# A fused attention, MoE and feed-forward kernel: weight decoding loaded two steps ahead, its mask on POOL, and token transposes spread over PSUM banks

## The chip, the cores and the metric

The kernel runs on one core of one Trainium2 chip. The metric is the device time of one execution in microseconds (us). TensorE appears as PE (matmul) and PEld (loading of the stationary operand), VectorE as DVE, ScalarE as ACT, GpSimd as POOL and the engine that issues most transfers as SP. Each of them works through its own instructions in the order in which they were written; semaphores hold an instruction back until its operands and its buffer are there.

## The reference, cut to what matters

Three layers follow one another on 2304 tokens of 512 values: windowed attention, a top-2 mixture of 8 experts, and a feed-forward layer with a piecewise gate. The change touches only what surrounds the last two.

```python
def _moe_ref(x, w_gate, w_noise, noise, w1, w2):        # N, D = 2304, 512; E, F = 8, 1024
    ...
    for e in range(E):
        for k in range(2):
            mask = top2[:, k] == e
            ...
            h = np.maximum(x[mask] @ w1[e], 0.0)
            out[mask] += top2_w[mask, k, None] * (h @ w2[e])

def _moe2_ref(x, w_in, w_out):                          # 512 -> 2048 -> 512
    h = x @ w_in
    g = np.where(h >= 1, h, np.where(h <= -1, 0.0, (h + 1) ** 2 / 4.0))
    return g @ w_out
```

The two matrices of the last layer, `w_in` and `w_out`, arrive as 64-bit floats. [...]

## The kernel before, in words

**Stages.** Attention comes first (to about 107 us of the span), with the router's choice of experts. Then the experts run one after another, each with up to 640 tokens that a gather by POOL brings in: unit 0 and 1 (one expert in two parts), units 2 to 7 (one expert each, called e1 to e6; the sorted lists get shorter, from 640 to 544 tokens), a small unit of 64 spilled tokens (`SPILL`), and units 7a and 7b. Last come five groups of the feed-forward layer, g0 with 256 tokens and g1 to g4 with 512 each. g0 multiplies plainly (`plain`); from g1 on each block is computed by a scheme with seven products in place of eight (`wino`), for which sums of blocks of `w_in` were prepared and stored earlier.

**A step.** Inside an expert the loop runs over 8 chunks of the hidden layer. PE computes `mm1` of the next chunk (L863) and then `mm2` of this one (L926). Matmuls run with 32-bit values cut in a high and a low part, three products for each. So for every chunk ACT writes the high part and DVE the rest, of the hidden values (`act_relu`: ReLU at L871, subtraction at L874) and of the weights (`split_w`: L157, L158). `mm1` writes into two PSUM banks; the next `mm1` may start when L871 and L874 have read them. The transpose of the next expert's tokens (L743 on PE, L746 and L747) goes between the two.

**Decoding.** While units 2 to 6 run, seven of every eight steps also decode 128x512 numbers, 32 pieces in all. `dec_load` (L174, SP) brings the raw integers into one of two buffers `rawd`. `dec_a` makes a mask `dm` on ACT that is positive where the number is not too small (L182 Abs, L183 Sign). `dec_b` has five DVE operations (L195, L197, L199, L200, L201), of which L199 takes the larger of mask and zero and multiplies by it, and a POOL addition (L203) that writes `td`. In the loop `dec_a` is issued ahead of the next chunk's `mm1` and its ReLU; `dec_b` and the next `dec_load` come at the end of the step, and the load of piece i+1 is issued in the step that decodes piece i.

**Sums and stores.** After every fourth piece a list `todo` gets ten entries: four POOL sums (L220, in two entries) and eight splits (L236 on ACT, L237 on DVE). `prepare(3)` in each step issues the stores of what is ready (L246, SP) and then three entries. The tiles of these sums, the masks, the gathered tokens and the results that are scattered all rotate through one pool `sc` with ten buffers.

**From g0 to g1.** The tokens of the next group are two rows each, y1 and y2 (one per chosen expert). `prep_mix` scales both on ACT (L1027, L1028) and adds them on POOL (L1029). `xcopy` transposes 128 tokens with four PE operations (L1222), always into bank 7 (`TR`), and ACT copies them out (L1226). `xsums` (L1236) and `xsplit` (L1245, L1246) make the operands of `wino`, and the table `AT` says at which place of a step: entry (p, j) is step p of the group and position j of seven. The gate of g0 (`act_gate`: L881 to L888) goes back and forth between ACT and DVE for each of two chunks.

What follows are the functions that the change touches and those that call them.

## Time and profile before

| what | value |
|---|---|
| three timed runs | 999.34, 999.82, 1005.02 us (median 999.82) |
| the profiled execution | 992.05 us, of which the span from first to last instruction is 990.3 us |
| PE, PEld busy | 950.4 us (96%), 841.4 us |
| DVE, ACT, POOL busy | 656.5 us (66%), 441.7 us (45%), 223.7 us (23%) |
| mean granted TensorE clock | 0.988 of full speed |
| moved by DMA | 201 MB, mean 203 GB/s |

A busy PE says that matmuls are under way, not that they run at their best speed. A row "idle before X <- Y" says how long the engine of X stood before it and which event ended that. The granted clock is given as a share of full speed: 1.00 is the upper of the two levels (2.4 GHz) and 0.50 the lower (1.2 GHz).

### The profile page before, as it was taken

How to read it: one execution, taken by the hardware profiler on the slowest of the kernel's cores; microseconds unless marked ns; L12 is line 12 of the kernel's file. 1: busy time of each engine (PE TensorE's matmuls, PEld its weight loads, DVE VectorE, ACT ScalarE, POOL GpSimd, SP SyncE). 2: the span in 40 equal slices, each digit the busy share in tenths (PEclk: the TensorE clock that was granted, in tenths of full speed). 3: DMA queues.
4: the chain of work that ended last, by engine and by line, in shares of the span. 5: the costliest groups of instructions: out<-in, count | busy, mean ns of one | idle time of the engine just before them, and what ended most of it. 6: DMA issues, size and time to landing. Idle time of an engine off the chain costs nothing. (4 is left out here: it accounts for less than half of the span.)

```text
span 990.3 us, 18428 instructions
## 1 busy us (share of the span) xinstructions
PE 950.4 (96%) x6917; PEld 841.4 (85%) x6918; DVE 656.5 (66%) x1386; ACT 441.7 (45%) x910; POOL 223.7 (23%) x275
## 2 busy tenths in 40 slices
PE   8998899999998989899999998899999999999998
PEld 6887789998987879789888887798899899889897
DVE  4689476586976878777442264775766676576664
ACT  6987224455564444554332254344334333433222
POOL 3212112345244344432402022112101300210000
PEclk9999999999999989989999999999999999999999
DMA  8874126568767876776927265485567558556531
GB/s 257 279 245 153 54 97 187 210 196 279 256 214 250 261 269 210 245 258 199 346 93 252 92 223 213 146 305 165 170 209 263 167 171 294 174 170 206 183 123 42
DMA packets 92796, 201.17 MB, mean 203 GB/s; under 512 B 7432, under 2 KB 17928, under 8 KB 92704
## 3 DMA queue, kind: packets, MB, share of 16 engines
q1 hardware_dynamic: 85264, 177.84, 54.6%
q0 software_dynamic: 6144, 19.76, 5.5%
q10 hardware_dynamic: 1296, 2.36, 0.6%
q8 instruction: 55, 0.90, 0.4%
q14 instruction: 37, 0.30, 0.1%
HBM read 159.65 MB, written 40.29 MB: 202 GB/s over the span
## 5 line engine op out<-in xcount | busy, mean ns | idle before, releaser
L926 PE MATMUL bank<-wo,hg 128*128 128x512 f32 x864 | 240.3, 397 | 0.0
L926 PE MATMUL bank<-w,he 128*128 128x512 f32 (+3 forms) x696 | 170.4, 396 | 0.0
L926 PEld LDWEIGHTS bank<-wo,hg 128*128 128x128 f32 x864 | 148.1, 190 | 17.6
L926 PEld LDWEIGHTS bank<-w,he 128*128 128x128 f32 (+3 forms) x696 | 124.7, 184 | 26.7
L863 PE MATMUL bank<-xhie,w 128*128 128x288 f32 (+4 forms) x768 | 125.4, 307 | 12.7 <-DVE he L874 12.7
L863 PEld LDWEIGHTS bank<-xhie,w 128*128 128x128 f32 x768 | 115.4, 194 | 21.4 <-DVE he L874 17.1
L158 DVE TENSOR_TENSOR w<-raw,w 128x1024 fp32r<-128x1024 f32 (+1 forms) x71 | 80.9, 1139 | 24.8 <-ACT w L157 24.5
L1168 PEld LDWEIGHTS bank<-xb,wi 128*128 128x128 f32 x576 | 80.4, 188 | 12.6 <-ACT r L881 2.3
L874 DVE SCALAR_TENSOR_TENSOR he<-bank,he 128x320 fp32r<-128x320 f32 (+8 forms) x120 | 43.3, 401 | 67.5 <-ACT he L871 67.4
L1168 PE MATMUL bank<-xb,wi 128*128 128x256 f32 x576 | 84.9, 283 | 2.6 <-ACT r L881 1.7
L1192 ACT ACTIVATE hg<-cg 128x512 fp32r<-128x512 f32 x64 | 40.3, 629 | 100.6 <-DVE cg L1190 100.6
L1168 PEld LDWEIGHTS bank<-xc,wi 128*128 128x128 f32 x480 | 67.2, 188 | 7.6 <-DVE wg L1153 0.6
L1168 PE MATMUL bank<-xc,wi 128*128 128x256 f32 x480 | 70.2, 281 | 0.2 <-DVE wg L1153 0.2
L157 ACT ACTIVATE w<-raw 128x1024 fp32r<-128x1024 f32 (+1 forms) x71 | 69.8, 983 | 0.0
L863 PE MATMUL bank<-xloe,w 128*128 128x288 f32 (+4 forms) x384 | 69.8, 304 | 0.0
L203 POOL TENSOR_TENSOR td<-rawd 128x512 f32<-128x512 f32 x32 | 33.3, 1039 | 158.3 <-DVE rawd L201 92.4
L871 ACT ACTIVATE he<-bank 128x288 fp32r<-128x288 f32 (+4 forms) x96 | 37.2, 412 | 65.4 <-PE bank L863 65.3
L1029 POOL TENSOR_TENSOR y<-y,y 128x512 f32<-128x512 f32 x15 | 20.5, 1363 | 200.4 <-ACT y L1028 200.4
L182 ACT ACTIVATE dm<-rawd 128x512 f32<-128x512 f32 x32 | 21.6, 675 | 90.5 <-DMA rawd<-wd 78.3
L1186 ACT ACTIVATE mg<-cg 128x512 f32<-128x512 f32 x64 | 40.1, 626 | 47.1 <-DVE cg L1158 45.4
L1187 DVE SCALAR_TENSOR_TENSOR cg<-mg,cg 128x512 f32<-128x512 f32 x64 | 47.0, 734 | 18.8 <-ACT mg L1186 18.8
L863 PEld LDWEIGHTS bank<-xloe,w 128*128 128x128 f32 x384 | 59.1, 193 | 0.0
(300 smaller groups left out, 1607.4 us busy)
## 6 DMA issues: line engine op xcount, KB each, us to landing
wi<-w1o SPq DMA_DIRECT2D x56, 1024.0 KB, 5.5
raw<-wcat SPq DMA_DIRECT2D x64, 512.0 KB, 4.3
rawd<-wd SPq DMA_DIRECT2D x32, 512.0 KB, 4.4
w1o<-so SPq DMA_DIRECT2D x64, 256.0 KB, 5.7
y<-y_dram SPq DMA_DIRECT2D x30, 256.0 KB, 5.3
vE<-v SPq DMA_DIRECT2D x18, 260.0 KB, 5.1
x_dram<-x SPq DMA_DIRECT2D x18, 256.0 KB, 2.3
k<-kT SPq DMA_DIRECT2D x8, 512.0 KB, 6.7
```

The source lines that it names most:

```text
L157: nc.scalar.activation(w[:, 0, c], t[:, c], AF.Copy)
L158: nc.vector.tensor_tensor(out=w[:, 1, c], in0=t[:, c], in1=w[:, 0, c].bitcast(F32), op=ALU.subtract)
L182: nc.scalar.activation(m, w, AF.Abs)
L203: nc.gpsimd.tensor_tensor(out=t, in0=hf, in1=lf, op=ALU.add)
L863: nc.tensor.matmul(ps, lhsT=l[k], rhs=r[:, k, s:s + w], start=(c == 0), stop=(c == len(prods) - 1))
L871: nc.scalar.activation(hh, ps, AF.Relu)
L874: nc.vector.scalar_tensor_tensor(out=t, in0=ps[:, c], scalar=0.0, in1=hh[:, c].bitcast(F32), op0=ALU.max, op1=ALU.subtract)
L926: nc.tensor.matmul(M2[b][0:w], lhsT=h2[:, o:o + w], rhs=r[n], start=(first and a == 0), stop=(last and a == end))
L1168: nc.tensor.matmul(ps, lhsT=w[:, l, k * P:k * P + P], rhs=r[:, m, k, :], start=(c == 0), stop=(c == len(prods) - 1))
L1186: nc.scalar.activation(st["m"], c, AF.Relu, scale=0.5)
L1187: nc.vector.scalar_tensor_tensor(out=c, in0=st["m"], scalar=1.0, in1=c, op0=ALU.min, op1=ALU.subtract)
L1192: nc.scalar.activation(h2[:, 0:T], c, AF.Copy, scale=-1.0)
```

## The change

The diff has five parts.

1. **Loads of the decoding.** Three `rawd` buffers in place of two. The first two pieces are loaded at the end of unit 1, and every decoding step begins with the stores that are ready and the load of piece i+2. `dec_a` is issued after the next chunk's `mm1` and ReLU.
2. **The mask.** ACT gets a third operation, a ReLU of the mask, so that it is 0 or 1. The DVE operation L199 is gone; POOL multiplies the finished piece by the mask in a second operation behind its addition. So ACT has one operation more for each of 32 pieces, DVE one fewer, POOL one more.
3. **Sums and stores.** Their tiles have a pool of their own, `so`, with six buffers. `todo` gets four entries per four pieces, one for each step, and every sum is split one step after POOL was told to make it.
4. **The weight ring** has 10 buffers in place of 12. The last two of the four pairs of the spill unit's chunks and two of the four `wi` tiles use a pool `we` in the place that the decoding's pools leave; those are closed in unit 7, not in `SPILL`. The last pair is loaded at chunk 5, not 4.
5. **From g0 on.** Transposes of even blocks go into bank 7, those of odd blocks into one of banks 2 to 6 that the group at work doesn't use. For g1 alone the mix is one ACT scaling and one DVE operation. The first two splits for g1 no longer wait for the sums and stand at (4, 0) and (4, 2).

```diff
-RING = 12
-PAIRS = (0, 1, 3, 4)
+RING = 10
+PAIRS = (0, 1, 3, 5)
...
+    def stream(k, shape, dt, name):
+        return ring.tile(shape, dt, tag="w", name=name) if k < 2 else pool["we"].tile(shape, dt, tag=f"w{k}", name=name)
+
     def load_raw(n, eng=nc.sync):
         if SP <= n < NCE:
 
             if n % 2 == 0:
-                pool["pair"] = ring.tile([P, 2, 1024], F32, tag="w", name=f"w{n}")
+                pool["pair"] = stream((n - SP) // 2, [P, 2, 1024], F32, f"w{n}")
...
         nc.scalar.activation(m, w, AF.Abs)
         nc.scalar.activation(m, m, AF.Sign, bias=tiny[:, 0:1])
+        nc.scalar.activation(m, m, AF.Relu)
         d64[i] = (d64[i], m)
 
     def dec_b(i):
...
-            nc.vector.scalar_tensor_tensor(out=hf, in0=m, scalar=0.0, in1=hf, op0=ALU.max, op1=ALU.mult)
...
             nc.gpsimd.tensor_tensor(out=t, in0=hf, in1=lf, op=ALU.add)
+            nc.gpsimd.tensor_tensor(out=t, in0=t, in1=m, op=ALU.mult)
...
         def add(j, x, y, op):
-            o[j] = pool["sc"].tile([P, 2, 256], F32, tag="s", name=f"so{p}_{j}")
+            o[j] = pool["so"].tile([P, 2, 256], F32, tag="so", name=f"so{p}_{j}")
...
-        todo.extend((first, second))
-        for j, src in ((5, None), (2, None), (3, None), (6, None), (0, a11), (1, a12), (4, a22), (7, a21)):
-            todo.append(lambda j=j, src=src: split(j, src))
+        def cut(*js):
+            for j in js:
+                split(j, {0: a11, 1: a12, 4: a22, 7: a21}.get(j))
+        todo.extend((lambda: (first(), cut(0, 1)), lambda: (second(), cut(5, 2)), lambda: cut(3, 6), lambda: cut(4, 7)))
...
             nc.scalar.activation(y1, y1, AF.Copy, scale=wts[:, t, 0:1])
-            nc.scalar.activation(y2, y2, AF.Copy, scale=wts[:, t, 1:2])
-            nc.gpsimd.tensor_tensor(out=y2, in0=y2, in1=y1, op=ALU.add)
+            if un is units[FIRST2 + 1]:
+                nc.vector.scalar_tensor_tensor(out=y2, in0=y2, scalar=wts[:, t, 1:2], in1=y1, op0=ALU.mult, op1=ALU.add)
+            else:
+                nc.scalar.activation(y2, y2, AF.Copy, scale=wts[:, t, 1:2])
+                nc.gpsimd.tensor_tensor(out=y2, in0=y2, in1=y1, op=ALU.add)
...
     def xcopy(ui, b):
         un = units[ui]
         t = gat.pop((un["key"], b))
+        free = [x for x in bank[2:7] if x not in units[ui - 1]["m2"]]
+        TR = bank[7] if b % 2 == 0 else free[b // 2 % len(free)]
...
         decode = 1 < ui < E - 1 and f <= 6
+        if ui == 1 and f > 5:
+            dec_load(ndl)
+            ndl += 1
+        if decode and ndl < n64:
+            prepare(0)
+            dec_load(ndl)
+            ndl += 1
...
         if ui == 1 and f == 2:
-            pool["rd"] = dec.enter_context(tc.tile_pool(name="rd", bufs=2, reuse_waits="tile"))
-            pool["td"] = dec.enter_context(tc.tile_pool(name="td", bufs=4, reuse_waits="tile"))
+            for x, k in (("rd", 3), ("td", 4), ("so", 6)):
+                pool[x] = dec.enter_context(tc.tile_pool(name=x, bufs=k, reuse_waits="tile"))
...
-        if decode and ndec < min(ndl, n64):
-            dec_a(ndec)
...
             do_mm1(ndone)
             ndone += 1
+        if decode and ndec < n64:
+            dec_a(ndec)
...
         if decode:
-            prepare(3)
-            if ndec < min(ndl, n64):
+            prepare(1)
+            if ndec < n64:
                 dec_b(ndec)
                 ndec += 1
-            if ndl < n64:
-                dec_load(ndl)
-                ndl += 1
         elif todo or stores:
-            prepare(3)
+            prepare(1)
+        if ui == SPILL - 1 and f == 2:
+            assert not todo and not stores
+            dec.close()
+            pool["we"] = ffn.enter_context(tc.tile_pool(name="we", bufs=1, reuse_waits="tile"))
...
-          {(4, 4): (None,), (4, 5): (0,), (4, 6): (1,), (5, 0): (2,), (5, 2): (3,), (5, 4): (4,), (5, 5): (5,), (5, 6): (6,)})
+          {(4, 0): (0,), (4, 2): (1,), (4, 4): (None,), (5, 0): (2,), (5, 1): (3,), (5, 3): (4,), (5, 4): (5,), (5, 6): (6,)})
```

On SP the load of the piece moves ahead of the step's weight load, and it is one piece further on. This is the step of unit 3 that has mask `dm8` on ACT (`rawd` raw integers, `raw` expert weights, `w1o` and `w2o` the stored results, `so` and `td` their tiles). Before:

```order
L174 DMA rawd8_3572<-wd 128x1024
L144 ISA
L144 DMA raw27_3634<-wcat 128x1024
L246 DMA w1o_71<-so1_5_3555 128x512
L246 DMA w2o_72<-td7_3565 128x512
L174 DMA rawd9_3651<-wd 128x1024
```

With the change:

```order
L251 DMA w1o_71<-so1_5_3462 128x512
L251 DMA w1o_71<-so1_2_3464 128x512
L251 DMA w2o_72<-td7_3539 128x512
L177 DMA rawd10_3549<-wd 128x1024
L147 ISA
L147 DMA raw26_3604<-wcat 128x1024
```

Piece 8 is now followed by the load of piece 10, still behind the stores of what was finished just before, and ahead of the weights.

On ACT, in the same step (`he` the hidden values, `w` the weight split), before:

```order
L182 ACTIVATE dm8_3576<-rawd8_3572 128x512
L183 ACTIVATE dm8_3576<-dm8_3576,tiny_110 128x512
L871 ACTIVATE he2_19_3579<-bank0_73 128x316
L871 ACTIVATE he2_19_3579<-bank1_74 128x316
L746 ACTIVATE xhie3_3608<-bank7_78 128x4x128
L157 ACTIVATE w25_3631<-raw25_3489 128x1024
```

With the change:

```order
L876 ACTIVATE he2_18_3553<-bank0_73 128x316
L876 ACTIVATE he2_18_3553<-bank1_74 128x316
L185 ACTIVATE dm8_3582<-rawd8_3307 128x512
L186 ACTIVATE dm8_3582<-dm8_3582,tiny_110 128x512
L187 ACTIVATE dm8_3582<-dm8_3582 128x512
L160 ACTIVATE w24_3601<-raw24_3448 128x1024
```

The mask has moved from ahead of the two ReLUs to between them and the weight split, and has three operations.

On PE, in step 3 of g0 (`y` the mixed tokens, `wo`, `hg` the operands of `mm2`), before:

```order
L1222 MATMUL bank7_78<-idn_164,y2_7108 128x128 x4
L926 MATMUL bank2_75<-wo3_6913,hg0_78_7187 128x512 x2
L926 MATMUL bank3_76<-wo3_6913,hg0_78_7187 128x512 x2
L1222 MATMUL bank7_78<-idn_164,y3_7111 128x128 x4
L926 MATMUL bank3_76<-wo3_6913,hg0_78_7187 128x512
```

With the change:

```order
L1232 MATMUL bank7_78<-idn_164,y2_7147 128x128 x4
L931 MATMUL bank2_75<-wo3_6952,hg0_78_7226 128x512 x2
L931 MATMUL bank3_76<-wo3_6952,hg0_78_7226 128x512 x2
L1232 MATMUL bank4_2118<-idn_164,y3_7150 128x128 x4
L931 MATMUL bank3_76<-wo3_6952,hg0_78_7226 128x512
```

The places are the same; the second block's transpose goes to bank 4.

## Rows read from the trace of the kernel before

**Rows 1.** Windows, decoding units and unit 7: us; busy PE, PEld, DVE, ACT, POOL; clock; DMA; GB/s.

```profile
225.00:466.00 241.00, 228.28 (x1315) 202.97 (x1314) 185.04 (x335) 122.03 (x238) 96.37 (x95) 0.97 0.74 243
466.00:512.00 46.00, 46.00 (x287) 40.76 (x286) 20.20 (x38) 16.18 (x29) 11.23 (x11) 1.00 0.73 250
```

**Rows 2.** Waits on PE and ACT, 225 to 466 us: total us, times, longest.

```profile
PE bank L863 <- DVE he L874: 12.7, 9, 3.3
ACT dm L182 <- DMA rawd<-wd: 64.0, 17, 7.8
```

**Rows 3.** Timeline around one stall, 302 to 307 us: start, duration, engine, instruction, idle before.

```profile
302.22 0.45 SPq L174 DMA_DIRECT2D rawd<-wd  x1
...
304.13 0.66 ACT L182 ACTIVATE dm<-rawd 128x512 f32<-128x512 f32 x1 [7.81 <-DMA rawd<-wd]
...
305.45 0.72 ACT L871 ACTIVATE he<-bank 128x304 fp32r<-128x304 f32 x2
...
306.42 1.38 PE L863 MATMUL bank<-xhie,w 128*128 128x304 f32 x8 [2.23 <-DVE he L874]
```

**Rows 4.** Windows over the three half-clock stretches of the decoding: the first, and their sum.

```profile
366.00:372.80 6.80, 5.48 (x23) 5.48 (x24) 5.50 (x11) 4.04 (x8) 1.19 (x3) 0.50 0.92 295
...
sum 13.60, PE 12.13 PEld 12.13 DVE 11.65 ACT 7.25 POOL 2.12; mean PE 4.04 PEld 4.04 DVE 3.88 ACT 2.42 POOL 0.71
```

**Rows 5.** Groups by line, 225 to 466 us: count, busy us, mean ns, idle before.

```profile
L183 ACT ACTIVATE dm<-dm,tiny 128x512 f32<-128x512 f32 x26 | 18.8, 724 | 0.8
L182 ACT ACTIVATE dm<-rawd 128x512 f32<-128x512 f32 x26 | 17.5, 674 | 76.2 <-DMA rawd<-wd 64.0 <-DVE rawd L201 6.8 <-DMA y_dram<-ye,rank_i 3.5
...
L199 DVE SCALAR_TENSOR_TENSOR rawd<-dm,rawd 128x512 f32<-128x512 f32 x27 | 18.7, 694 | 0.9
...
L200 DVE TENSOR_SCALAR td<-rawd 128x512 int32<-128x512 int32 x27 | 11.5, 427 | 0.9
...
L203 POOL TENSOR_TENSOR td<-rawd 128x512 f32<-128x512 f32 x27 | 28.1, 1039 | 130.1 <-DVE rawd L201 64.1 <-DMA raw<-wcat 18.4 <-issue 16.7
```

**Rows 6.** Transfers into the decoding's buffers, 225 to 466 us.

```profile
DMA to landing us min/median/max: 3.5/4.5/8.2
```

**Rows 7.** Timeline of a step with a late DVE, 384 to 391 us.

```profile
384.84 0.92 POOL L220 TENSOR_TENSOR so<-td,so 128x256 f32<-128x256 f32 x1
...
385.08 0.96 DVE L195 TENSOR_SCALAR td<-rawd 128x512 int32<-128x512 int32 x1
...
386.80 0.41 ACT L871 ACTIVATE he<-bank 128x288 fp32r<-128x288 f32 x1 [0.75 <-PE bank L863]
...
388.60 0.88 DVE L874 SCALAR_TENSOR_TENSOR he<-bank,he 128x288 fp32r<-128x288 f32 x3
...
390.20 1.08 PE L863 MATMUL bank<-xhie,w 128*128 128x288 f32 x7
```

**Rows 8.** Timeline of g0, 604 to 622 us: mix, transposes and their copies.

```profile
604.73 0.71 ACT L1028 ACTIVATE y<-y,wts 128x512 f32<-128x512 f32 x1
...
610.41 0.58 ACT L1226 ACTIVATE xhis<-bank 128x512 f32<-128x512 f32 x1
...
611.09 0.63 PE L1222 MATMUL bank<-idn,y 128*128 128x128 f32 x4 [3.77 <-issue]
...
621.22 0.63 PE L1222 MATMUL bank<-idn,y 128*128 128x128 f32 x4 [1.90 <-ACT xhis L1226]
```

**Rows 9.** Windows over the two half-clock stretches of g0.

```profile
611.80:615.20 3.40, 3.40 (x12) 2.85 (x11) 0.00 (x0) 2.11 (x4) 2.44 (x2) 0.50 0.00 0
622.00:625.40 3.40, 3.40 (x12) 2.81 (x11) 2.85 (x3) 1.52 (x3) 2.21 (x2) 0.50 0.12 44
```

**Rows 10.** Timeline of the end of g0, 614 to 640 us: gate on ACT, first `wino` products.

```profile
616.34 0.38 ACT L881 ACTIVATE r<-bank 128x256 f32<-128x256 f32 x1 [2.42 <-PE bank L863]
...
626.47 0.39 ACT L881 ACTIVATE r<-bank 128x256 f32<-128x256 f32 x1 [2.95 <-PE bank L863]
...
636.36 0.98 PE L1168 MATMUL bank<-xb,wi 128*128 128x256 f32 x6 [1.42 <-ACT r L881]
```

## What the change should do to the time

> **What bounds the kernel now.** I read the windows first, to see where PE stands idle. In units 3 to 6, which decode, PE is busy for 228.28 of 241 us; in unit 7, which has the same steps but no decoding, for 46.00 of 46 [rows 1]. So PE's own work sets the pace, and the decoding units lose 12.7 us on top of it. The waits say to whom: all 12.7 us, in nine waits, are an `mm1` that waits until DVE has read its bank (L874) [rows 2]. DVE was late because ACT was: over the same stretch ACT stood 64.0 us in front of the mask's first operation, waiting for the raw integers [rows 2]. The timeline shows one case from end to end: ACT idles 7.81 us before L182, only then comes the ReLU (L871) of an `mm1` that had long ended, and PE starts the next one 2.23 us late [rows 3].
>
> Idle time has a second price. After these waits come stretches in which the granted clock is 0.50, the lower level: 13.60 us in three places, with 12.13 us of matmuls in them [rows 4]. At the upper level these would take half, so the stretches cost about 12.13 / 2 = 6.1 us.
>
> The second place is g0. Two transposes of the next group's tokens wait 3.77 and 1.90 us, since bank 7 still holds the block before, which ACT copies out only at 610.41 behind the gate's long chain [rows 8]. Two stretches of 3.40 us at half clock follow [rows 9] and cost 6.80 / 2 = 3.4 us. Sum: 5.7 + 3.4 = 9.1 us. Elsewhere the change touches nothing on which PE waits noticeably.
>
> **The change, part by part.**
>
> *Loads and the place of the mask.* The raw integers land 3.5 to 8.2 us after their issue [rows 6]. The stretch of 241 us holds 32 steps; without its losses a step takes (241 - 18.8) / 32 = 6.9 us. One step ahead is therefore not enough when the load issues late, two steps (13.9 us) are. On SP the load now stands behind the stores that are ready; one of them, in every second step, waits for POOL's addition and multiplication of the piece before, 2 x 1.04 us after DVE is done with it [rows 5]. If that delays the issue by 4 us, an estimate of mine from DVE's lateness below and these 2.1 us, 9.9 us are left against at most 8.2. The weight load behind it moves later by as much, with two steps of its own in hand. And since the mask now follows the ReLU, a late load no longer holds the ReLU. So I let all nine waits go: 12.7 us, and with them the half clock, 6.1 us: 18.8 us.
>
> *What is late next.* Between ReLU and weight split ACT now has three operations: 0.674 + 0.724 us and a third that the trace lacks in this shape. Its nearest rows are those two, so 0.67 to 0.72; I take 0.70 [rows 5]. ACT's weight split, and with it DVE's half of it, the splits of the sums and the decoding, start 2.1 us later after the ReLU; DVE's part is shorter by L199, 0.694 us [rows 5]. So DVE reaches the next L874 up to 1.4 us later than now. How late may it be? In the step of [rows 7] L874 starts 1.8 us after the ReLU's start, ends at 389.48, and PE's next `mm1` starts at 390.20 without idling: 0.7 us were left, so lateness is free up to 2.5 us. A punctual L874 starts 0.4 us after the ReLU (the ReLU takes 0.41 us there); plus 1.4 makes 1.8, which is inside.
>
> *The mask on POOL.* 32 multiplications at the addition's 1.039 us [rows 5] are 33 us more on POOL, which is busy 96.37 of 241 us [rows 1]. They hide there; gathers behind them start 1 us later and have two steps. But POOL can hold DVE up: L195, which normally takes as long as its like L200, 0.427 us [rows 5], took 0.96 us while a POOL sum ran, 0.53 us more [rows 7]. One such hold leaves 0.2 us of DVE's margin, two overdraw it by 0.35 us. The multiplication follows the addition directly, when DVE is done with the piece, so it meets a DVE operation less often than the sums do. Bounds: no hold, 0 us; two holds in every one of 32 steps, 32 x 0.35 = 11 us. I take two holds in eight of the 16 steps that make sums: 2.8 us.
>
> The Trainium skill (SBUF — State Buffer, section "SBUF: two separate sides") is sterner: DVE and GpSimd take a shared port pair as an exclusive lock for a whole instruction, and the loser blocks fully. By that every multiplication may hold DVE 1.04 us, 33 us in all, and if all of it reached PE the time would be some 1010 us. The row of [rows 7] agrees that DVE stops; it shows 0.53 us for one meeting, since POOL had begun before.
>
> *Sums, own buffers, ring of 10.* One entry per step and splits a step after the sums take ACT's and DVE's waits for POOL away; they cost nothing, with the same operations as before. The stores' own six buffers relieve `sc`; a buffer of `so` is wanted again three steps after its tile was begun, one step after its store was issued. A weight buffer in a ring of 10 is written again three steps after its last use, where it was five; nobody waits. The two loads that move to the end of unit 1 add no bytes; at worst one landing, 4.5 us, shows once. I take 0.
>
> *g0.* With banks of their own the two transposes need not wait: 5.7 us, and the half clock with it, 9.1 us. What is late next is ACT. PE comes 9.1 us earlier to the end of g0; ACT saves four scalings of 0.71 us [rows 8], 2.8 us, and had 2.42 + 2.95 us of waiting for PE [rows 10], together 8.2 us. The missing 0.9 us come back where `wino` starts, which already waits 1.42 us for ACT's gate [rows 10]; about as much again for the second bank, whose gate half follows the first. I take 1.8 us. Bounds: 0.9 and all 9.1. The four DVE mixes, bounded by 0.694 us each as an operation of the same kind [rows 5], replace POOL's work off the path.
>
> **Sum.** Decoding 18.8 - 2.8 = 16.0 us, g0 9.1 - 1.8 = 7.3 us, together 23.3 us. The profiled execution took 992.05 us (span 990.3), so the changed kernel would take 968.8 in such a profile. The three timed runs have a median of 999.82, 7.8 us more than the profiled one; I know of no reason why the stalls should be different there, so the same difference gives 976.5 us.
>
> **The rivals.**
>
> *DVE becomes the bound (slower).* If POOL's addition and multiplication hold DVE for their full 2.1 us in each step, L874 is 1.8 + 2.1 = 3.9 us late, 1.4 us beyond the free 2.5. PE then waits 32 x 1.4 = 45 us in place of 12.7, the half clock stays, g0 still gains 7.3: 999.8 + 45 - 12.7 - 7.3 = 1025 us. It decides from 2.5 us of lateness on. For it: DVE is busy 185 of 241 us [rows 1], and the hold exists [rows 7]. Against it: POOL starts the pair only after DVE's last operation on the piece, and the next on DVE is L874, which reads a PSUM bank that POOL doesn't use. That is the same port rule that the Trainium skill states in SBUF — State Buffer.
>
> *Half of the decoding's waits stay,* because ACT now waits elsewhere (for POOL's sums, for a store to leave a buffer): 8 + 7.3 us gained, 984.5 us. For it: ACT and POOL are chained more tightly than before. Against it: every chained pair has a whole step between its ends.
>
> *g0 gains nothing:* the bound of 9.1 us given back, so 16.0 us gained, 983.8 us. For it: ACT's chain there is serial, and its share of the slack is used up.
>
> *The change doesn't do what it says:* the load, still behind a store that waits for POOL, lands late in spite of its two steps, and the mask holds up the weight split as it once held the ReLU. Only g0 gains: 992.5 us. The 8.2 us landing [rows 6] speaks for it, the 1.7 us in hand against.
>
> **How the numbers follow.** The forecast has 0.58, half of the waits 0.13, g0 without gain 0.12, the load still late 0.08, DVE as the bound 0.06; 0.03 is for what I don't see. The forecast's own bounds: all of 18.8 and 9.1 and the 1.42 us at `wino` gained, 29.3 us, 970.5 us; 11 us of holds and 1.8 given back, 984.7. The range takes in the next two cases and part of the last but one, and below, since the profile and the runs differ by 0.8%, 4 us more: 966 to 991 us. A measurement here can tell about 1%, 10 us, from no change: faster is below 989.8. That holds in the first three cases but for a little: 0.81. Within 1%: the late load and the edges, 0.13. Slower: 0.06.
>
> **What would show it.** Right: in units 3 to 6 PE idles under 4 us, ACT's wait for raw integers no longer ends a chain that reaches PE, the clock reads 1.00 throughout, and the transposes of g0 show no idle time. The first two `wino` products then wait longer than now. Wrong: `mm1` waits for L874's successor in many steps, with DVE operations near 1 us while POOL multiplies; or SP's loads still land after ACT asks for them; or POOL's gathers come too late for the next expert's transposes.

## The result, and where its 11 us come from

The changed kernel takes 988.8 us (median of four runs: 988.92, 991.36, 988.70, 987.57), the kernel before 1000.3 us (999.34, 999.82, 1005.02, 1000.75). The ratio is 0.9879 with a 95% interval of 0.9842 to 0.9916: 11.5 us, or 1.2%, faster. The forecast was 976.5 us in a range of 966 to 991: the sign and the range held, half of the forecast gain came. The profiled execution of the changed kernel took 988.92 us (span 986.9).

Line numbers are those of each kernel's own file: the ReLU that is L871 in the kernel before is L876 in the changed one, the subtraction behind it L879 instead of L874, `mm1` L868 instead of L863, and each experiment shifts them by a line or a few. Decoding is the work that turns the 64-bit weights into 32-bit floats.

To see where, I matched the traces. TensorE's matmuls fall into 839 runs of one source line each, in every trace of this study, so the same run can be timed in all of them. That cuts the span into stages:

| stage | before | changed | forecast |
|---|---|---|---|
| until unit 3 | 225.4 us | 226.6 us | same |
| units 3 to 6 (decoding) | 241.0 | 235.0 | 225.0 |
| unit 7, with the spill unit's first 16 matmuls | 56.6 | 56.6 | same |
| rest of the spill unit, units 7a and 7b | 67.9 | 74.1 | same |
| g0 and the first three products of g1 | 48.8 | 43.7 | 41.5 |
| from there to the end | 350.6 | 351.1 | same |

Three things differ from the forecast: decoding gained 6.0 us, not 16.0; g0 5.1, not 7.3; and a stage that the change was not to touch became 6.2 us longer. The last one explains why the profiles differ by only 3 us where the timed runs differ by 11.5, and it turns out below not to be the change's doing: a kernel that equals the one before up to that place has it too.

**Decoding.** Windows over units 3 to 6 and unit 7 of the changed kernel, columns as in [rows 1]:

```profile
226.60:461.60 235.00, 225.78 (x1315) 201.56 (x1314) 181.42 (x304) 139.19 (x262) 142.27 (x121) 0.98 0.74 248
461.60:507.00 45.40, 45.40 (x284) 40.31 (x283) 19.24 (x34) 15.87 (x28) 11.89 (x11) 1.00 0.69 239
```

PE still loses 9.2 us to idling, and POOL's busy time has gone from 96 to 142 us. The waits of the same stretch (engine, what it waited for, total us, times, longest):

```profile
PE bank L868 <- DVE he L879: 9.0, 4, 5.2
ACT so L240 <- POOL so L224: 6.7, 4, 3.5
DVE so L241 <- POOL so L224: 18.5, 8, 7.4
```

The wait for raw integers that led [rows 2] with 64.0 us is gone. In its place the splits of the sums (L240 on ACT, L241 on DVE) wait for POOL's sums (L224), and PE's four waits for `he` are fewer than the nine before, but longer. (`so` are the sums, `ye` the experts' results that POOL scatters, `xge` the tokens that it gathers.) The timeline shows the longest from end to end (start, duration, engine, instruction, idle before):

```profile
408.96 2.25 POOL L910 DMA_INDIRECT y_dram<-ye,rank_i  x1
...
410.17 0.41 ACT L876 ACTIVATE he<-bank 128x288 fp32r<-128x288 f32 x1 [1.00 <-PE bank L868]
...
415.34 0.91 POOL L910 DMA_INDIRECT y_dram<-ye,rank_i  x1 [0.31 <-issue]
416.27 0.74 POOL L224 TENSOR_TENSOR so<-td,td 128x256 f32<-128x256 f32 x1
416.95 0.73 POOL L224 TENSOR_TENSOR so<-td,so 128x256 f32<-128x256 f32 x1
...
417.72 0.42 DVE L241 TENSOR_TENSOR so<-so 128x256 fp32r<-128x256 f32 x1 [7.42 <-POOL so L224]
...
418.06 0.88 DVE L879 SCALAR_TENSOR_TENSOR he<-bank,he 128x288 fp32r<-128x288 f32 x3
418.57 2.29 PE L868 MATMUL bank<-xhie,w 128*128 128x288 f32 x8 [5.22 <-DVE he L879]
```

An expert's last step puts five scatters (L910) on POOL, from 408.96 to 416.25, and the two sums stand behind them. DVE meets the split of these sums (L241) before it meets L879, which would read the bank that PE needs; the ReLU for it began at 410.17. So DVE stands for 7.42 us, and PE for 5.22. Two smaller cases have a gather (L840) ahead of the sums, at 247 us (PE 2.3 us) and 384 us (1.2 us); ahead of the second DVE had also been held in its weight split (2.18 us at 378.42, shown further below).

**The half clock** in the changed kernel, windows over its four places (decoding twice; the spill unit; the start of g1):

```profile
249.60:253.00 3.40, 3.35 (x13) 3.35 (x14) 3.40 (x5) 0.00 (x0) 3.17 (x3) 0.54 0.00 0
...
416.90:423.70 6.80, 5.13 (x21) 5.13 (x22) 5.54 (x12) 1.25 (x3) 2.57 (x4) 0.52 0.74 215
...
522.90:529.70 6.80, 5.23 (x72) 4.59 (x74) 0.00 (x0) 0.77 (x2) 0.12 (x1) 0.50 0.08 24
628.50:635.30 6.80, 5.77 (x22) 5.01 (x23) 4.50 (x12) 1.80 (x6) 0.00 (x0) 0.52 0.31 120
```

Each begins during a wait of PE or right behind one (2.32, 5.22, 4.58 and 2.95 us). Decoding has 3.4 + 6.8 = 10.2 us at the lower level where [rows 4] had 13.6; in a second profile of the changed kernel (below) the same two places have 3.4 us each.

**g0.** Timeline of its end, the counterpart of [rows 8, 10]:

```profile
613.57 0.60 PE L1232 MATMUL bank<-idn,y 128*128 128x128 f32 x4
...
614.94 0.60 PE L1232 MATMUL bank<-idn,y 128*128 128x128 f32 x4
...
625.97 1.13 ACT L1255 ACTIVATE xb<-xlos 128x512 fp32r<-128x512 f32 x2
...
627.01 1.13 ACT L1255 ACTIVATE xa<-xlos 128x512 fp32r<-128x512 f32 x2
...
628.04 0.61 ACT L1255 ACTIVATE xa<-xhis 128x512 fp32r<-128x512 f32 x1
...
628.57 0.36 ACT L886 ACTIVATE r<-bank 128x256 f32<-128x256 f32 x1
...
628.98 1.65 PE L1176 MATMUL bank<-xb,wi 128*128 128x256 f32 x6 [2.95 <-ACT r L886]
...
631.61 1.65 PE L1176 MATMUL bank<-xb,wi 128*128 128x256 f32 x6 [0.55 <-ACT r L886]
```

The transposes no longer wait: the 3.77 and 1.90 us of [rows 8] are gone. But ACT does five splits (L1255) in a row right ahead of the gate's ReLU (L886) that frees the bank of the first product of g1, so PE waits 2.95 us there, where it waited 1.42 [rows 10], and 6.8 us at half clock follow.

### The profile page after: what moved, and what is told of

Read it like the earlier page. It is cut to its first block, busy times and chain, and to the rows that moved or that the text cites. A ratio compares the mean times of both kernels' runs of the same rounds, so it can differ in the third digit from the quotient of the medians.

```text
span 986.9 us, 18441 instructions
## 1 busy us (share of the span) xinstructions
PE 949.9 (96%) x6918; PEld 841.7 (85%) x6918; DVE 653.2 (66%) x1358; ACT 461.3 (47%) x938; POOL 271.9 (28%) x303
## 5 line engine op out<-in xcount | busy, mean ns | idle before, releaser
L868 PE MATMUL bank<-xhie,w 128*128 128x288 f32 (+4 forms) x768 | 123.9, 304 | 9.1 <-DVE he L879 9.0
L868 PEld LDWEIGHTS bank<-xhie,w 128*128 128x128 f32 x768 | 114.5, 192 | 16.6 <-DVE he L879 11.7
L161 DVE TENSOR_TENSOR w<-raw,w 128x1024 fp32r<-128x1024 f32 (+1 forms) x71 | 95.0, 1338 | 39.1 <-ACT w L160 37.0
L876 ACT ACTIVATE he<-bank 128x288 fp32r<-128x288 f32 (+4 forms) x96 | 40.2, 420 | 132.2 <-PE bank L868 129.7
L868 PE MATMUL bank<-xloe,w 128*128 128x288 f32 (+4 forms) x384 | 69.2, 303 | 0.0
L879 DVE SCALAR_TENSOR_TENSOR he<-bank,he 128x320 fp32r<-128x320 f32 (+8 forms) x120 | 43.4, 400 | 31.4 <-ACT he L876 26.6
L1195 DVE SCALAR_TENSOR_TENSOR cg<-mg,cg 128x512 f32<-128x512 f32 x64 | 47.0, 734 | 18.8 <-ACT mg L1194 18.8
L868 PEld LDWEIGHTS bank<-xloe,w 128*128 128x128 f32 x384 | 58.6, 192 | 0.0
L1204 DVE SCALAR_TENSOR_TENSOR hg<-cg,hg 128x512 fp32r<-128x512 f32 x64 | 46.0, 718 | 9.1 <-ACT hg L1200 8.7
```

Of the source, the lines that this page charges most:

```text
L161: nc.vector.tensor_tensor(out=w[:, 1, c], in0=t[:, c], in1=w[:, 0, c].bitcast(F32), op=ALU.subtract)
L868: nc.tensor.matmul(ps, lhsT=l[k], rhs=r[:, k, s:s + w], start=(c == 0), stop=(c == len(prods) - 1))
L876: nc.scalar.activation(hh, ps, AF.Relu)
L879: nc.vector.scalar_tensor_tensor(out=t, in0=ps[:, c], scalar=0.0, in1=hh[:, c].bitcast(F32), op0=ALU.max, op1=ALU.subtract)
L1195: nc.vector.scalar_tensor_tensor(out=c, in0=st["m"], scalar=1.0, in1=c, op0=ALU.min, op1=ALU.subtract)
L1204: nc.vector.scalar_tensor_tensor(out=h2[:, T:2 * T], in0=c, scalar=-1.0, in1=h2[:, 0:T].bitcast(F32), op0=ALU.mult, op1=ALU.subtract)
```

## The experiments

Twelve kernels ran, in three series; the kernels of one series ran on one chip, together with the kernel before, and each series on another chip. The kernel before took 993.87 us in the first series, 1000.12 in the second and 1000.39 in the third, so ratios are compared across series, and times only within one. The stages were cut as above, each from the one execution that was profiled. For "spill ReLU on DVE" that was its slowest (984.54 us), so its stages are not held against the others'.

| kernel | us | ratio to before, 95% | units 3 to 6 | spill, 7a, 7b | g0 |
|---|---|---|---|---|---|
| first series, before 993.87 | | | | | |
| before again | 992.60 | 0.9985 [0.9966, 1.0003] | 239.9 | 67.8 | 48.8 |
| sums first | 969.56 | 0.9756 [0.9735, 0.9776] | 221.6 | 67.8 | 43.6 |
| mask on DVE | 973.08 | 0.9782 [0.9759, 0.9805] | 223.8 | 67.9 | 43.9 |
| 16 operations on ACT | 983.35 | 0.9893 [0.9873, 0.9912] | 234.1 | 67.7 | 43.9 |
| second series, before 1000.12 | | | | | |
| changed again | 990.11 | 0.9909 [0.9882, 0.9936] | 234.1 | 73.1 | 43.6 |
| g0 part alone | 992.60 | 0.9930 [0.9903, 0.9957] | 239.1 | 74.2 | 43.8 |
| loads and g0 only | 981.34 | 0.9818 [0.9788, 0.9848] | 224.1 | 73.1 | 43.9 |
| sums first, splits later in g0 | 976.70 | 0.9771 [0.9745, 0.9796] | 221.9 | 74.0 | 43.6 |
| third series, before 1000.39 | | | | | |
| sums first again | 977.90 | 0.9781 [0.9758, 0.9805] | 222.6 | 73.7 | 43.5 |
| sums first, spill ReLU on DVE | 978.68 | 0.9783 [0.9757, 0.9810] | 225.4 | 74.5 | 44.2 |
| sums first, 16 operations on ACT | 978.30 | 0.9774 [0.9751, 0.9797] | 222.6 | 74.1 | 43.8 |
| sums first, mask on DVE | 976.61 | 0.9752 [0.9729, 0.9776] | 220.5 | 73.1 | 43.9 |

### Decoding: what holds DVE up

**Sums first.** POOL's sums are issued at the top of their step, ahead of gather and scatters; the splits stay.

```diff
-        todo.extend((lambda: (first(), cut(0, 1)), lambda: (second(), cut(5, 2)), lambda: cut(3, 6), lambda: cut(4, 7)))
+        todo.extend(((first, lambda: cut(0, 1)), (second, lambda: cut(5, 2)), (int, lambda: cut(3, 6)),
+                     (int, lambda: cut(4, 7))))
...
-                todo.popleft()()
+                todo.popleft()[1]()
...
             dec_load(ndl)
             ndl += 1
+        if todo:
+            todo[0][0]()
```

Expected: 

> The changed kernel with POOL's two sums issued at the top of their step, ahead of the gather and the five scatters; the splits stay where they are. Theory (the splits of the sums wait since POOL has the sums behind gathers and scatters): DVE's 20.5 us and ACT's 6.7 us of waiting for the sums nearly vanish, PE's waits for he in decoding fall from 9.0 to under 2 us, the half-clock stretches of 6.8 and 3.4 us there go, and the time falls by 7 to 12 us, to some 978. Rival (DVE is late because POOL holds it while it multiplies): the waits of PE stay at 7 us or more and the time stays within 3 us.

Measured: ratio 0.9756; units 3 to 6 take 221.6 us instead of 234 to 235. Windows over them, and the waits that are left there:

```profile
227.60:449.10 221.50, 220.82 (x1314) 197.92 (x1313) 175.94 (x304) 138.89 (x262) 142.39 (x120) 1.00 0.78 263
```

```profile
PE bank L749 <- DMA xge<-x_dram,rank_i: 0.6, 1, 0.6
...
DVE so L241 <- POOL so L224: 5.2, 5, 2.0
```

The clock reads 1.00, no wait for `he` is left, and DVE's waiting for the sums fell from 18.5 to 5.2 us. The same place in the timeline:

```profile
403.37 2.15 POOL L224 TENSOR_TENSOR so<-td,td 128x256 f32<-128x256 f32 x1
...
405.48 0.73 POOL L224 TENSOR_TENSOR so<-td,so 128x256 f32<-128x256 f32 x1
406.25 0.42 DVE L241 TENSOR_TENSOR so<-so 128x256 fp32r<-128x256 f32 x1 [1.33 <-POOL so L224]
406.38 1.20 POOL L911 DMA_INDIRECT y_dram<-ye,rank_i  x1 [0.16 <-issue]
...
407.81 1.22 PE L869 MATMUL bank<-xhie,w 128*128 128x288 f32 x8
```

The sums are now ahead of the first scatter, DVE waits 1.33 us and PE not at all. The theory's numbers hold, but for DVE's waits for the sums, which fell to a quarter and did not nearly vanish; the rival's don't hold. The stage gains 12.5 to 13.4 us on the two profiles of the changed kernel, a little more than the 7 to 12 expected.

**Mask on DVE.** The multiplication goes back to DVE in one operation (L199 of before); ACT's third operation and POOL's second are left out.

```diff
-        nc.scalar.activation(m, m, AF.Relu)
...
+            nc.vector.scalar_tensor_tensor(out=hf, in0=m, scalar=0.0, in1=hf, op0=ALU.max, op1=ALU.mult)
...
-            nc.gpsimd.tensor_tensor(out=t, in0=t, in1=m, op=ALU.mult)
```

Expected: 

> The changed kernel with the mask's multiplication back on DVE in one operation and without the third operation on ACT and the second on POOL. If POOL's multiplication holds DVE up (weight split L161 1.14 to 1.34 us), L161 falls back to about 1.15 us, PE's 9.0 us of waits in decoding fall below 4, and the time falls by 5 us or more. If the sums behind gathers and scatters are the cause, the longest wait (5.2 us behind five scatters) stays, POOL is freed of about 1.5 us per step, so waits of 6 to 8 us remain and the time stays within 4 us. ACT has 32 instructions fewer before the spill unit: if the 4.1 us there hang on where ACT's instructions are fetched, they go too.

Measured: ratio 0.9782. Windows and waits of the decoding units:

```profile
229.10:452.90 223.80, 221.16 (x1315) 197.90 (x1314) 183.83 (x330) 122.85 (x235) 95.71 (x94) 1.00 0.78 260
```

```profile
PE bank L867 <- DVE he L878: 2.6, 2, 2.1
...
DVE so L240 <- POOL so L223: 9.8, 5, 4.5
```

Here my expectation for late sums was wrong: with the sums still behind the scatters I let 6 to 8 us of waits remain, and 2.6 remain, as the other expectation (POOL holds DVE) had it. DVE's weight split fell too, from 1.50 to 1.30 us at 1024 columns (the 1.34 and 1.14 us of the expectation are means over both of its widths). This run does not tell the two apart, since the edit does two things: POOL is busy 95.7 us here instead of 142, so it comes to the scatters and to the sums behind them sooner, and no multiplication can hold DVE. What it shows is that either remedy, the sums ahead or the multiplications gone, takes nearly all of the loss away. What the multiplications cost when the sums are not late is told by the next two.

**Sums first and mask on DVE**, both edits together, beside **sums first again** on the same chip.

Expected: 

> The kernel with the sums first and the mask's multiplication back on DVE in one operation, without ACT's third and POOL's second one. If POOL's multiplication costs time of its own (DVE's weight split was 1.34 us with it, 1.14 us in the kernel before), the time falls by 2 us or more; if DVE's slack covers it, as in the kernel with the sums first where PE has no wait left in decoding, the time is the same within 2 us.

Measured: 976.61 against 977.90 us, ratios 0.9752 and 0.9781 with intervals that overlap. The stage shows it better: 220.5 us against 221.6 to 222.6 with the sums first alone.

```profile
228.90:449.40 220.50, 220.50 (x1315) 198.11 (x1314) 181.85 (x330) 122.59 (x235) 97.71 (x94) 1.00 0.78 263
```

PE is busy for all of the 220.5 us. So POOL's multiplication costs 1 to 2 us once its queue is in order. DVE is not the way by which it costs them: with the sums first PE never waits for DVE in these units, but once, 0.6 us (first series) and 1.1 us (third), for gathered tokens (L749 above), which come through POOL's longer queue; with the mask on DVE that wait is gone. The ratio is the lowest of all, though its interval overlaps that of the sums first alone.

**Loads and g0 only.** The loads two steps ahead, the ring of 10 and the g0 part; mask and its place ahead of the ReLU, sums, splits and buffers as in the kernel before.

```diff
-        if decode and ndec < n64:
-            dec_a(ndec)
         if s == len(seq) - 1:
...
                     prep_xpose(x, b)
+        if decode and ndec < n64:
+            dec_a(ndec)
...
-            prepare(1)
+            prepare(3)
```

Expected: 

> The changed kernel with the loads two steps ahead, the ring of 10 and the g0 part, but the mask on DVE and ACT ahead of the ReLU as before, the sums and their splits by the old list of three entries per step, in the common buffers. If the late loads alone caused the stalls of decoding (12.7 us and 6.1 us at half clock), all of these go: 0.975 to 0.98 of the kernel before, as fast as the kernel with the sums first, and ACT's 64 us of waiting for raw integers fall under 10. If the chain of mask, sums and splits on ACT, DVE and POOL is what makes PE wait even with punctual loads, at least 4 us of waits for he stay and the ratio is 0.983 to 0.99.

Measured: 981.34 us, 8.8 us less than the changed kernel in the same series; the intervals of the ratios (0.9788 to 0.9848, 0.9882 to 0.9936) are apart. Windows and waits of the decoding units:

```profile
227.10:451.20 224.10, 220.96 (x1315) 198.10 (x1314) 184.58 (x327) 122.96 (x234) 98.07 (x94) 1.00 0.76 258
```

```profile
PE bank L866 <- DVE he L877: 3.1, 2, 1.6
...
ACT so L239 <- POOL so L223: 7.7, 5, 4.2
```

No wait for raw integers is in ACT's list any more (one of 5.0 us ahead of the mask is left, put down to a scatter). Against the 239.1 us of this stage in the kernel with the g0 part alone, the loads, with the ring of 10, take 15.0 us away; mask, sums and splits, as the change has them, give 10 of these back.

### The 4.1 us ahead of the spill unit's ReLU

In the profile of the changed kernel, and not in that of before, ACT's first ReLU of the spill unit (L974) starts 4.12 us late, PE waits 4.58 us for it, and the half clock follows. Here is the place in the second profile of the kernel before (first series), and in the changed kernel ("remote": no instruction in the trace matches the event that ended the wait):

```profile
523.78 1.62 PE L965 MATMUL bank<-xsp,w 128*64 128x64 f32 x48
525.51 0.38 ACT L969 ACTIVATE hsp<-bank 128x256 f32<-128x256 f32 x1
525.95 2.08 PE L965 MATMUL bank<-xsp,w 128*64 128x64 f32 x64 [0.54 <-ACT hsp L969]
```

```profile
518.11 1.62 PE L970 MATMUL bank<-xsp,w 128*64 128x64 f32 x48
523.87 0.38 ACT L974 ACTIVATE hsp<-bank 128x256 f32<-128x256 f32 x1 [4.12 <-remote]
524.31 3.68 PE L970 MATMUL bank<-xsp,w 128*64 128x64 f32 x64 [4.58 <-ACT hsp L974]
```

My first theory was that ACT waits there for its own next instructions, since the change gives it 32 more ahead of this place. **16 operations on ACT** moves them on:

```diff
+        if ui == SPILL - 1 and 2 <= f <= 5:
+            for _ in range(4):
+                nc.scalar.activation(idle, tiny, AF.Copy)
```

Expected: 

> The changed kernel with 16 copies of one column on ACT in unit 7, which nothing uses: they only move ACT's later instructions on. Theory (ACT waits 4.1 us ahead of the spill unit's ReLU for its own next instructions, which are fetched at that place): the 4.1 us vanish there or turn up elsewhere, PE's 4.6 us of idle time and the 6.8 us at half clock behind it go, and the time falls by 4 to 8 us. Rival (the ReLU waits for the pair loads or a buffer, which come later by the other order of the loads): the 4.1 us stay, and the time stays or rises by up to 1 us.

Measured: the wait is absent and the ratio is 0.9893, no better than the changed kernel's 0.988 and 0.991. That told nothing, for the wait is absent from all four kernels of that series, **before again** among them, and one of them has as many ACT instructions as the changed kernel.

Expected of the kernel before: 

> The kernel before, unchanged, with a profile of its own. The timed runs before had a median of 1000.3 us, the one profile 992.1. If runs in a series are longer than a profiled execution by about 8 us, this profile reads about 992 again with the same nine waits of PE (12.7 us in units 3 to 6). Rival: the stalls differ from execution to execution, and then this profile reads nearer to 1000 and shows more or longer waits than the first one.

Measured: 992.60 us in the runs and 992.67 in the profile, as in the first profile (992.05), though the first runs took 1000; units 3 to 6 take 239.9 us against 241.0. Runs are not longer than a profiled execution as such, and the stalls of decoding are the same from one execution to the next. The second series began with the **changed kernel again**.

Expected: 

> The changed kernel unchanged, with a profile of its own, on the chip of the other runs of this call. If ACT's 4.1 us ahead of the spill unit's ReLU belong to the program (its place in the instructions, a buffer), they stand in this profile too. If they come and go with the execution, as their absence in a kernel with the same number of ACT instructions hints, they are likely gone, and the profile reads about 5 to 8 us less than the timed runs of a case with them. The time: 0.988 of the kernel before, within 0.004.

Measured: 0.9909, and the wait is there (4.15 us), against my guess that it would be gone. It is there in all four kernels of that series, the one with the **g0 part alone** included, which is the kernel before up to this place.

Expected of that one: 

> The kernel before with the g0 part alone (four banks for the transposes, sums of the tokens' mixes on DVE, splits earlier). Nothing before g0 changes. By the prediction 7.3 us less than the kernel before; by the changed kernel's trace, where ACT's five splits ahead of the gate cost 2.95 + 0.55 us and a half-clock stretch, 5 us less. Rival: 0 to 2 us, if the gain in the trace of the changed kernel came from the different arrival of PE at g0.

Its ratio of 0.9930 is 7.0 us with an interval of 4.3 to 9.7, which holds both values expected. The stage tells them apart: g0 takes 43.8 us against 48.8, 5.0 less, and so it does within 0.6 us in every kernel with this part (43.5 to 44.2 us). The five splits' wait and the half clock behind it are in its trace too.

In the third series **sums first again** was the measure for two edits at this place.

Expected: 

> The kernel with the sums first once more, as the measure for the others of this call. ACT's wait of 4.1 us ahead of the spill unit's ReLU stood in four kernels of the last call and in none of the first, whatever their edits. If it goes with the chip and not with the program: where the kernel before has a median of about 1000 us in this call it stands here too, the time is about 976 and the ratio 0.976; where the kernel before has about 994 it is absent and the time is about 970. Rival (it goes with the program): absent as in this kernel's first profile, whatever the time of the kernel before.

Measured: the wait is there, which it was not for the same kernel in the first series; the kernel before takes 1000.39 us. So it goes with the series and not with the program; whether with the chip, or with where the program lies on it, is not shown. With **16 operations on ACT** it is there too:

Expected: 

> The kernel with the sums first and 16 unused copies of one column on ACT in unit 7, which move ACT's later instructions on. If the wait ahead of the spill unit's ReLU depends on where ACT's instructions lie, it is gone here though the kernel with the sums first has it (5 to 8 us less); if not, both have it or neither, and the times are the same within 2 us.

Measured: 978.30 against 977.90 us, the wait at 4.20 us. And with the **spill ReLU on DVE**:

```diff
-            nc.scalar.activation(hbuf["sp"][:, sl], ps[:, sl], AF.Relu)
+            nc.vector.tensor_scalar(out=hbuf["sp"][:, sl], in0=ps[:, sl], scalar1=0.0, scalar2=None, op0=ALU.max)
```

Expected: 

> The kernel with the sums first, and the spill unit's two ReLUs on DVE instead of ACT. If the wait at that place belongs to ACT alone, PE no longer waits 4.6 us there and loses no half clock behind it: where the kernel with the sums first has the wait, 5 to 8 us less than that; where it has none, the same time within 2 us. Rival (all engines stand still there): DVE's ReLU is as late as ACT's, the time is the same in either case.

Measured: 978.68 us, no gain. In its timeline DVE now is what is late:

```profile
514.86 0.22 PE L971 MATMUL bank<-xsp,w 128*64 128x64 f32 x1 [0.37 <-issue]
...
518.72 0.42 DVE L975 TENSOR_SCALAR hsp<-bank 128x256 f32<-128x256 f32 x1 [2.94 <-remote]
519.20 3.63 PE L971 MATMUL bank<-xsp,w 128*64 128x64 f32 x64 [4.12 <-DVE hsp L975]
```

So it isn't ACT, and not its instructions. What both wait for is PE's signal: among the trace's semaphore events PE's counter rises at 523.79 us in the changed kernel, just ahead of ACT's start at 523.87, though the last of the matmuls is recorded by 519.7; in the second profile of before it rises at 525.42, 0.02 us after the matmuls' end. All 64 matmuls of this half (16 and 48) are in both traces, so none is hidden in the gap, and other engines go on: POOL starts a scatter at 522.15 us. A transfer of instructions (16 KB) starts within 0.7 us of the start of the 48 matmuls shown, in all 14 profiles, and is over 2 us after that start, with the wait and without it, so it doesn't tell them apart. Why PE's signal comes 4 us late in some series, I have not found out. In 14 profiles it stands or falls with the series: five without it (the first profile of before and the four of the first series), nine with it.

### g0

**Sums first, splits later in g0.** The last two splits stand behind the ReLU of the next gate.

```diff
                 for x in AT[late].get((p, j), ()):
+                    if late and x in (5, 6):
+                        fill.append(lambda ui=ui, x=x: xsplit(ui + 1, x))
+                        continue
                     xsums(ui + 1) if x is None else xsplit(ui + 1, x)
```

Expected: 

> The changed kernel with the sums first and, in g0, the last two splits of the tokens' sums put behind the ReLU of the next gate instead of ahead of it. In g0 PE's wait at the first product of the next group (3.1 us with five splits ahead) falls by the two splits' 1.2 us to about 1.8, the second product's wait rises by up to 1 us since DVE's part of the two splits now stands inside the gate's chain. If the 6.8 us at half clock go too: 4 to 5 us less than with the sums first alone (ratio 0.971); if they stay: within 1 us of it (0.9755).

Measured: ratio 0.9771, stage g0 43.6 us, both as without the edit. Its timeline at the start of g1:

```profile
615.67 0.36 ACT L887 ACTIVATE r<-bank 128x256 f32<-128x256 f32 x1
...
615.94 0.62 ACT L1256 ACTIVATE xa<-xlos 128x512 fp32r<-128x512 f32 x1
...
616.09 1.07 PE L1177 MATMUL bank<-xb,wi 128*128 128x256 f32 x6 [1.91 <-ACT r L887]
...
619.37 0.36 ACT L887 ACTIVATE r<-bank 128x256 f32<-128x256 f32 x1
619.78 1.65 PE L1177 MATMUL bank<-xb,wi 128*128 128x256 f32 x6 [2.20 <-ACT r L887]
```

The first product's wait fell to 1.91 us as expected, the second's rose from 0.55 to 2.20, more than the 1 us expected, and the half clock stayed. The two waits together are 4.1 us instead of 3.5: what bounds PE here seems to be ACT's and DVE's whole chain, not where in it the splits stand; a run with a shorter chain was not made.

## Why the prediction came out at half its gain

**Loads: right.** With the old mask, sums and splits left in place, the earlier loads turn PE's nine waits for DVE (12.7 us) into two (3.1 us), the integers no longer appear among ACT's waits, and this experiment gains 15.0 us in the stage by itself, of the 18.8 that I had put down for all of decoding's losses. The rival of the late load (992.5 us) is out.

**Half clock: right that it goes with the long waits.** With the sums first the clock reads 1.00 in the four units; in the changed kernel, with waits of up to 5.2 us, it does not. Shorter waits need not bring one: with the mask on DVE 2.6 us remain, 2.1 us at most, and it reads 1.00.

**Sums and splits: the step that failed.** The prediction had "One entry per step and splits a step after the sums take ACT's and DVE's waits for POOL away; they cost nothing", and set against its second rival "every chained pair has a whole step between its ends". A step of 6.9 us is enough only where POOL has nothing ahead of the sums. Ahead of them it has a gather in most steps and five scatters, 7.3 us, in an expert's last. I had put POOL's queue into the sum for the gathers behind the multiplications and not for the sums behind the gathers and scatters, nor asked who stands behind the split on DVE: L879, which PE waits for. This took 10 of the forecast 16 us; shown by undoing it alone, which gives 221.6 us where 225.0 were forecast. It takes both, the sums' place and POOL's multiplications: without the multiplications, and with the sums where they were, the stage takes 223.8 us. The rival that came true is the second, "Half of the decoding's waits stay", which let 8 us of decoding's losses go; 6.0 went. It named ACT as the engine that waits; the one that held PE up was DVE.

**Mask on POOL: the cost on the path was priced about right, its terms and the queue were not.** The hold exists. Two lines of the changed kernel over the whole trace (count, then shortest, median and longest ns), the weight split in the groups by line (count, busy us, mean ns, idle before), and one meeting in the timeline:

```profile
L207 POOL TENSOR_TENSOR td<-td,dm x32: 1282/1297/2135, 187.8 to 448.2; 128x512 f32<-128x512 f32 x32
...
L161 DVE TENSOR_TENSOR w<-raw,w x71: 670/1226/2291, 20.4 to 537.4; 128x1024 fp32r<-128x1024 f32 x57, 128x512 fp32r<-128x512 f32 x14
```

```profile
L161 DVE TENSOR_TENSOR w<-raw,w 128x1024 fp32r<-128x1024 f32 x57 | 85.4, 1497 | 32.9 <-ACT w L160 30.8 <-ACT ye L940 1.5 <-issue 0.5
```

```profile
378.23 1.30 POOL L207 TENSOR_TENSOR td<-td,dm 128x512 f32<-128x512 f32 x1
...
378.42 2.18 DVE L161 TENSOR_TENSOR w<-raw,w 128x1024 fp32r<-128x1024 f32 x1
```

The multiplication takes 1.30 us in 31 of 32 cases, not the 1.04 of the addition of the same shape that the forecast took for it [rows 5]. That is its own time and no hold: it takes 1.29 us also at 256.61 us, where DVE does nothing beside it. What is held is DVE's split of 1024 columns: 1.23 us in the median, 2.18 and up to 2.29 us where a multiplication runs beside it. Such a meeting costs up to 1.07 us, twice the 0.53 us of the forecast, and in units 3 to 6 a multiplication overlaps a split by 0.25 us or more in 16 of 27 cases. The mean of the split is 1.50 us in the changed kernel, 1.38 with the sums first and 1.27 with the mask on DVE as well. Most of this lands in DVE's slack: the forecast priced it at 2.8 us, and with POOL's queue in order the whole multiplication costs 1 to 2, part of them by a late gather. How much of the changed kernel's 9.0 us the holds add on top of the late sums no run tells apart. But 32 multiplications of 1.3 us also lengthen the queue ahead of the sums, and this the prediction let "hide there". The Trainium skill says of DVE and GpSimd that moving operations between the two might not help, since they share a port (Perfetto Trace Analysis, "Optimizing Scalar/DVE Operations"). The runs agree here: with the sums first, the mask costs nothing more on DVE than on POOL, 976.6 against 977.9 us. The rival with DVE as the bound at 1025 us is out.

**Loads at the end of unit 1, ring of 10, stores' own buffers: nothing, as forecast.** Unit 3 begins 226.6 us after the start, in the profiles of the kernel before at 225.4 and 227.3.

**g0: right, with its half clock mis-sized.** The transposes' 5.7 us went. Of the forecast's 3.4 us of half clock little came: two stretches of 3.4 us, with 6.80 us of matmuls [rows 9], became one of 6.8 with 5.77 us of them, behind the longer wait at the start of g1, where I had put a longer wait and no clock behind it. 1.5 us more of waiting there (2.95 against 1.42) were forecast as 1.8. The gain is 5.1 us instead of 7.3.

**The step from profile to runs: right in size, its reason unknown then.** I carried the 7.8 us between the profiled execution of before and its runs over to the changed kernel, without a reason. The late signal is the likely one: series with it show 1000 us for the kernel before, the series without it 994, and the stage with it is 5 to 7 us longer. That the first runs had it is inferred from their time, not seen.

**The sum.** Like with like, decoding's 6.0 and g0's 5.1 are 11.1 us; 11.5 were timed. With the sums first the same change gives 22 to 24 us (0.9756 to 0.9781), the 23.3 that the forecast had. That the sums agree is in part luck: in the profiles decoding then gains 17 to 19 us instead of 16.0, and g0 some 5 instead of 7.3.

**The signs.** Of the signs that the prediction named for being right, the transposes without idle time, the raw integers that no longer hold PE up and the longer waits of the first `wino` products came. PE's idle time under 4 us in units 3 to 6 (9.2) and a clock of 1.00 throughout (0.98) did not.

## What to carry over

When a step's operations are spread over engines that work in order, check for every chained pair what else stands ahead of its first half in that engine's queue at the worst step, not in the usual one, and what stands behind its second half. An operation moved to an engine with much idle time still lengthens the queue there, and everything issued behind it comes later; issue first what another engine waits for. And take a change apart: here the loads with the g0 part were faster than the whole.

## What the runs showed of the hardware

- PE's signal to the engine that reads its bank came 4.1 us late at one place, at the start of the spill unit, in every profile of two series and none of a third, with the same programs; with the half clock behind it that was 5 to 7 us, about half of what the change brought. Moving ACT's instructions, or giving the ReLU to DVE, did not touch it.
- A multiplication on POOL holds up DVE's subtraction of two SBUF tiles for most of the time that they share: 2.18 to 2.29 us instead of 1.23 where they overlap by 1.1 us or more. POOL's multiplication itself keeps its 1.30 us in 31 of 32 cases. DVE's copies out of PSUM are not held: 0.68 to 0.69 us in all twelve (L942), also where a multiplication runs beside them (294 us). No entry among the waits shows the hold, only the durations of the operations do.
